# Seven half-size products in place of eight in the second MLP matmul of a fused forgetting-attention and MLP kernel

## The chip, the cores and the metric

The kernel runs on one core of one Trainium2 chip. The metric is the device time of one launch in microseconds, the median over several runs. Besides the timed runs there is one profiled execution; its rows carry the line numbers of the kernel's source (L362 is line 362), the engine (PE is TensorE's matmul, PEld its weight load, DVE is VectorE, ACT is ScalarE, POOL is GpSimd, SP is SyncE), the tile written and the tiles read.

## What is computed

```python
# attention, for each of 8 batches and 8 heads, 576 tokens, head size 64
scores = q @ k.T / sqrt(D)
decay  = cum[:, None] - cum[None, :]          # cum = cumsum(log(clip(f, 1e-4, 1)))
attn   = softmax(causal(scores + decay))
x      = (attn @ v)                           # laid out as 4608 tokens x 512
# MLP
h   = x @ w_in                                # 512 -> 2048
g   = h - tanh(h)
out = g @ w_out                               # 2048 -> 512, float32
```

## The kernel before

Matmul operands are float16 and accumulate in float32 in PSUM. The attention works on 32 pairs of heads, four pairs for each of the eight batches. The MLP works on nine units of 512 tokens (`UW`), and a unit has two stages.

- `mlp1(u, ft)`, one item for each of the 16 blocks `ft` of 128 of the 2048 hidden columns: four matmuls of 128x512 into a PSUM bank `hps` (L352), tanh by ACT into `th` (L359), and an add by DVE that leaves the float16 block `gt` of 128 hidden columns by 512 tokens (L362). `hps` comes from the pool `ps_m`, three banks in rotation, so the matmuls of a block wait until the add of the block three earlier has read its bank. `th` comes from `tmp`, two buffers.
- `mlp2(u, s)`, 16 items of four matmuls: for each of four groups of 128 tokens, 16 matmuls of 128x512 accumulate in one bank of `ps_m` over the 16 blocks (`gt` is the stationary operand, a block of `wout` the moving one, L370). After the last, ACT copies the bank to `ost` (L374), and SP's queue stores 128 rows of the output.

An item of either stage is thus four 512-column matmuls. All items stand in one list (L433), unit after unit, each unit its 16 `mlp1` and then its 16 `mlp2`:

```python
mlp = [(fn, u, s) for u in range(NU) for fn in (mlp1, mlp2) for s in range(NFT)]
take = 0 if p < NPAIR else 3 if p == NPAIR else 7 if p <= 2 * NPAIR + 1 else 8
```

The order of the work on each engine is the order in which the program writes it (`manual_schedule`), and no engine changes it. The loop goes over the pairs `p` = 0 to 32, and each pair takes `take` items of the list and spreads them evenly between its own steps. The steps of a late pair are seven score tiles (`scores`, L273 on PE, exp by ACT on L287, causal masks by POOL on L297), `values` of the pair before (30 small matmuls on L308, then three DVE operations: L318, L319, L320) and `turn` (two transposing DMAs of SP that put the result in `XR`, the input of the first MLP matmul). What is left of the list after pair 32 runs at the end by itself.

From batch 3 on, q and k are transposed by DMA and laid out by eight copies of DVE (`place`, L95), which stand in the last pair of the batch before (p = 11, 15, 19, 23, 27): two after each of the first four score tiles. For earlier batches PE transposes (L237) and DVE copies from PSUM (L248), two copies for q and two for k in each pair up to p = 10.

`XR` is a ring over tokens, 4 batches of 576 long (L67, L326). A unit whose 512 tokens cross the end of the ring does each of its `mlp1` matmuls in two parts; with this length that is unit 4 alone, in two parts of 256 columns. The blocks `gt` have 22 buffers (L57). One PSUM bank, `ps_tr`, serves the early transposes and nothing later.

The lines that the change touches are the pools (L57), the ring (L67, L326), the start-up constants (L114 to L123, L155), `mlp1` (L355), the list (L433) and `take` (L441).

## Time and profile before

| | |
|---|---|
| median of 3 runs | 362.77 us (362.58 to 364.81) |
| span of the profiled execution, first to last instruction | 359.3 us |
| the executions' time over the span, taken from these two | 3.5 us |
| PE busy | 346.5 us, 96% of the span |
| ACT busy | 221.7 us, 62% |
| DVE busy | 199.1 us, 55% |
| POOL busy | 153.6 us, 43% |

The span is the profiled execution's own time; the timed runs also hold what lies around it. A row of a timeline gives the start, the time from there to the end of the last of the merged instructions, the engine, line and shapes, the count, and in brackets how long the engine had been idle and what ended that. A row of the groups gives the count, the busy time, the mean time of one instruction in ns, and the idle time before the group's instructions. Matmuls are pipelined: one takes longer from start to end than the distance to the next, so costs of matmuls are read from the starts.

### The profile page before, as it was taken

To read this page: it belongs to the slowest core of one execution; us is meant where nothing else is said; L and a number is where in the kernel's file an instruction comes from. 1 tells how busy PE (TensorE), PEld (TensorE's weight loads), DVE (VectorE), ACT (ScalarE), POOL (GpSimd) and SP (SyncE) were. 2 spreads that over 40 slices of the span, in tenths; PEclk is the share of its full clock that TensorE was granted. 3 is DMA by queue.
4 is the path that set the end of the run, shared out by engine and by line. 5 is a ranking of instruction groups with operands and counts; after the bars stand their busy time and mean duration, and the time that the engine had idled before them with its cause. 6 is when DMAs were issued, how large, how long until landed. Compare 5 with 4: busy or idle time off the path is not lost.

```text
span 359.3 us, 7490 instructions
## 1 busy us (share of the span) xinstructions
PE 346.5 (96%) x2792; PEld 190.3 (53%) x2792; DVE 199.1 (55%) x349; ACT 221.7 (62%) x416; POOL 153.6 (43%) x316
## 2 busy tenths in 40 slices
PE   7797899999999999999999999999999999999995
PEld 3475455555555555555557865555555554444442
DVE  8666799448961577157814781378127513802710
ACT  6567676558855785578657865686568734714611
POOL 8932463766276627762776267632222210000000
PEclk9789999999999999999999999999999999999999
DMA  7999999999799999999899969991220021011011
GB/s 118 158 188 187 208 194 80 118 145 161 96 102 151 168 97 76 149 181 112 66 144 153 143 65 147 151 156 35 76 75 16 18 77 61 0 60 58 0 48 71
DMA packets 140632, 38.74 MB, mean 108 GB/s; under 512 B 128004, under 2 KB 134900, under 8 KB 140596
## 3 DMA queue, kind: packets, MB, share of 16 engines
q0 software_dynamic: 92320, 18.36, 66.7%
q1 hardware_dynamic: 48276, 19.90, 29.2%
q8 instruction: 22, 0.36, 0.4%
q14 instruction: 14, 0.11, 0.1%
HBM read 36.85 MB, written 9.44 MB: 129 GB/s over the span
## 4 chain that ended last, share of the span: by engine, by line
PE 89%; DVE 6%; ACT 2%; DMA 1%; issue 1%; ACTq 0%
PE ops L370 35%; PE hps L352 32%; PE ps L273 12%; PE av L308 8%; ACT e L287 1%; DVE gt L362 1%; DVE QT L248 1%; DMA QT<-cqs 1%; PE t L237 1%; DVE xn L320 1%; PE ps L281 1%; DVE KT L248 0%; PE spin L226 0%; DVE cum L156 0%; ACT th L359 0%
## 5 line engine op out<-in xcount | busy, mean ns | idle before, releaser
L352 PE MATMUL hps<-XR,win 128*128 128x512 f16 (+1 forms) x640 | 140.9, 357 | 0.3 <-DVE gt L362 0.2
L370 PE MATMUL ops<-wout,gt 128*128 128x512 f16 x576 | 139.2, 378 | 0.0
L287 ACT ACTIVATE e<-ps 128x512 f16<-128x512 f32 x192 | 111.0, 596 | 39.6 <-PE ps L273 26.2
L362 DVE TENSOR_TENSOR gt<-hps,th 128x512 f16<-128x512 f32 x144 | 98.5, 689 | 58.4 <-ACT th L359 57.2
L297 POOL TENSOR_SCALAR_AFFINE_SELECT e<-e 128x128 f16<-128x128 f16 x168 | 56.6, 338 | 120.8 <-ACT e L287 120.5
L359 ACT ACTIVATE th<-hps 128x512 f32<-128x512 f32 x144 | 86.3, 599 | 33.0 <-PE hps L352 31.3
L352 PEld LDWEIGHTS <-win 128*128 128x128 f16 x640 | 57.9, 97 | 48.6 <-issue 0.7
L273 PE MATMUL ps<-QT,KT 67*128 67x64 f16 (+5 forms) x384 | 77.9, 281 | 3.9 <-ACT e L287 2.1
L370 PEld LDWEIGHTS <-gt 128*128 128x128 f16 x576 | 52.0, 97 | 52.6
L273 PEld LDWEIGHTS <-KT 67*128 67x128 f16 (+1 forms) x384 | 37.7, 99 | 41.2 <-issue 2.8
L374 ACT ACTIVATE ost<-ops 128x512 f32<-128x512 f32 x36 | 21.5, 597 | 54.3 <-PE ops L370 45.3
L318 DVE TENSOR_SCALAR rs<-av 128x10 f32<-128x10 f32 (+1 forms) x33 | 5.4, 163 | 69.3 <-PE av L308 69.3
L308 PEld LDWEIGHTS <-e 128*128 128x128 f16 x896 | 32.8, 98 | 7.5 <-issue 1.7
L308 PE MATMUL av<-vn,e 128*128 128x65 f16 x896 | 34.5, 194 | 1.0 <-DVE xn L320 1.0
L106 POOL DMA_DIRECT2D vn<-in_v_dram x32 | 28.4, 898 | 1.6 <-issue 0.8
L320 DVE TENSOR_TENSOR xn<-av,rs 128x640 f16<-128x640 f32 (+1 forms) x33 | 26.5, 804 | 1.1
L248 DVE COPY KT<-t 64x576 f16<-64x576 f16 (+1 forms) x26 | 19.5, 748 | 4.5 <-PE t L237 4.3
L87 POOL DMA_DIRECT2D qn<-in_q_dram x25 | 21.5, 859 | 0.8 <-issue 0.6
L87 POOL DMA_DIRECT2D kn<-in_k_dram x25 | 21.2, 850 | 1.1 <-issue 0.9
L248 DVE COPY QT<-t 64x576 f16<-64x576 f16 x22 | 17.6, 801 | 6.5 <-PE t L237 6.3
L308 PE MATMUL av<-vn,el 128*128 128x65 f16 x64 | 12.5, 195 | 0.0
L95 DVE COPY KT<-TK 64x1152 f16<-64x1152 f16 x20 | 11.4, 607 | 0.1
(58 smaller groups left out, 127.2 us busy)
## 6 DMA issues: line engine op xcount, KB each, us to landing
out_dram<-ost SPq DMA_DIRECT2D x36, 256.0 KB
vn<-in_v_dram POOLq DMA_DIRECT2D x32, 128.0 KB, 5.9
qn<-in_q_dram POOLq DMA_DIRECT2D x20, 128.0 KB, 3.7
kn<-in_k_dram POOLq DMA_DIRECT2D x20, 128.0 KB, 4.4
win<-in_moe_w_in_dram POOLq DMA_DIRECT2D x2, 1024.0 KB, 11.8
wout<-in_moe_w_out_dram POOLq DMA_DIRECT2D x2, 1024.0 KB, 17.4
XR<-xn SPq DMA_TRANSPOSE x56
qn<-in_q_dram POOLq DMA_DIRECT2D x1, 576.0 KB, 8.9
```

Source lines behind the costliest of these rows:

```text
L87: nc.gpsimd.dma_start(out=dst[b % 2][0:pn, n, :].rearrange("p (h d) -> p h d", h=H), in_=src[b, :, n * P:n * P + pn, :].rearrange("h p d - ...
L106: nc.gpsimd.dma_start(out=vn[b % 2][:, n, h0:h1, 0:D], in_=v[b, h0:h1, n * P:(n + 1) * P, :].rearrange("h p d -> p h d"))
L248: nc.vector.tensor_copy(out=to, in_=of)
L273: nc.tensor.matmul(out=ps[:, col:col + n], lhsT=KT[b % 2][0:rows, h, j * P:(j + 1) * P], rhs=QT[b % 2][0:rows, h, i0:i0 + n], start=True, ...
L287: nc.scalar.activation(out=e[:, lo:hi], in_=ps[:, lo:hi], func=AF.Exp, scale=qscale)
L297: nc.gpsimd.affine_select(out=view, in_=view, compare_op=ALU.is_ge, fill=0.0, base=0, pattern=pat, channel_multiplier=-1)
L308: nc.tensor.matmul(out=av[:, a, ib, :], lhsT=E.pop((b, c, a, j, ib)), rhs=vn[b % 2][:, j, 2 * c + a, 0:D + 1], start=(j == 0), stop=(j == ib))
L320: nc.vector.tensor_tensor(out=xn[:, :, h0 * D:(h0 + hn) * D].rearrange("p i (a d) -> p a i d", a=hn), in0=av[:, h0:h0 + hn, :, 0:D], in1=r ...
L352: nc.tensor.matmul(out=hps[:, o:o + n], lhsT=win[:, ci, ft * P:(ft + 1) * P], rhs=XR[:, ci, t:t + n], start=(ci == 0), stop=(ci == NCH - 1))
L359: nc.scalar.activation(out=th, in_=hps, func=AF.Tanh, scale=-1.0)
L362: nc.vector.tensor_tensor(out=gt, in0=hps, in1=th, op=ALU.add)
L370: nc.tensor.matmul(out=ops, lhsT=GT[(u, ft)][:, m * P:(m + 1) * P], rhs=wout[:, ft, :], start=(ft == 0), stop=(ft == NFT - 1))
```

## The change

The second matmul of units 1 to 8 is done by the scheme of Strassen in Winograd's form, once. The hidden columns, the unit's tokens and the output columns are each cut in halves, so that `gt` gives four quarters (A11 and A21 from blocks 0 to 7, for the first and the second 256 tokens; A12 and A22 from blocks 8 to 15) and `wout` four (B11, B12, B21, B22). Seven products of quarters or of sums of quarters take the place of eight. Unit 0 keeps `mlp2`.

- Sums of `wout`: four tiles `WS`, each by two DVE operations of 128x1024 float16, one in each of tiles 1 and 4 of the pairs p = 7 to 10. The tiles serve at first as room for start-up constants (`lf`, `cum`, `minus16`, `neg16`, `tri16`, `pick_k`).
- Sums of `gt`: `mlp1` of the blocks 8 to 15 has four more DVE operations behind its add, each 128x256 float16 with both inputs in SBUF: A11-A21, A21+A22 (written over A21), S2 = (A21+A22)-A11, and A12-S2. The third reads the second's result, the fourth the third's.
- The products: `product(u, n, g)` is eight matmuls of 128x256 for one group `g` of 128 tokens. Products 1, 6, 5, 3 are accumulated one on another in one bank (`ps_tr`, `px`), which ACT copies after 1, 6 and 5 to `part` and after 3 to `ost`. Product 2 has a bank of `ps_m`; products 7 and 4 share another, one on top of the other. For 2, 7 and 4 DVE adds the bank and a `part` (128x512 float32). Each of the four results is stored as 256 rows of 256 columns.
- The list: a unit has 30 items, not 32. Block 15 of `mlp1` comes after the first half of product 1, and the others follow in the order below. Even pairs from p = 10 on take 7 items, odd ones 8. Each unit therefore takes four pairs, always with the same place: of unit u, blocks 6 to 12 lie in p = 4u+6, and blocks 13 and 14, 1a, block 15, 1b, 2a, 6a, 6b lie in p = 4u+7 (a and b are the two groups). Units 7 and 8 run at the end, after the last pair.
- The ring `XR` holds three batches, so units 3 and 6 cross its end (192+320 and 384+128 columns). `gt` has 18 buffers.

```diff
-    gtp = ctx.enter_context(tc.tile_pool(name="gtp", bufs=NFT + 6))
+    gtp = ctx.enter_context(tc.tile_pool(name="gtp", bufs=NFT + 2))
+    smp = ctx.enter_context(tc.tile_pool(name="smp", bufs=NFT // 2 + 1))
+    prt = ctx.enter_context(tc.tile_pool(name="prt", bufs=3))
...
-    RING = 4 * S
+    K2, E2, T2 = NFT // 2, DM // 2, UW // 2
+    WS = [wpl.tile([P, K2, E2], FP16, tag=f"ws{i}", name=f"ws{i}") for i in range(4)]
+    RING = 3 * S
...
-    lf = cst.tile([NH, S], FP32)
+    lf = WS[0].rearrange("p k e -> p (k e)").bitcast(FP32)[0:NH, 0:S]
+    cum = WS[1].rearrange("p k e -> p (k e)").bitcast(FP32)[0:NH, 0:S]
...
-    neg16 = cst.tile([P, P], FP16)
-    tri16 = cst.tile([P, P], FP16)
+    neg16 = WS[3].rearrange("p k e -> p (k e)")[:, 512:640]
+    tri16 = WS[3].rearrange("p k e -> p (k e)")[:, 640:768]
...
-    minus16 = cst.tile([2 * H, S], FP16)
-    pick_k = cst.tile([P, 512], FP16)
+    minus16 = WS[2].rearrange("p k e -> p (k e)")[0:2 * H, 0:S]
+    pick_k = WS[3].rearrange("p k e -> p (k e)")[:, 0:512]
...
+    for n in range(4):
+        for i in range(2):
+            LOADS.setdefault((NPAIR + 3 + n, 1 + 3 * i), []).append(lambda n=n, i=i: wsum(n, i * K2 // 2, (i + 1) * K2 // 2))
...
+    def wsum(n, k0, k1):
+        dst, a, b = ((WT1, B12, B11), (WT3, B22, B12), (WT2, B22, WT1), (WT4, B21, WT2))[n]
+        nc.vector.tensor_tensor(out=dst[:, k0:k1, :], in0=a[:, k0:k1, :], in1=b[:, k0:k1, :], op=ALU.subtract)
...
-        r0 = b % 4 * S
+        r0 = b % 3 * S
...
         nc.vector.tensor_tensor(out=gt, in0=hps, in1=th, op=ALU.add)
+        if u == 0 or ft < K2:
+            return
+        k = ft - K2
+        a1, a2 = GT[(u, k)], gt
+        sm = smp.tile([P, 3, T2], FP16, tag="sm", name="sm")
+        SUM[(u, k)] = sm
+        nc.vector.tensor_tensor(out=sm[:, 0, :], in0=a1[:, 0:T2], in1=a1[:, T2:UW], op=ALU.subtract)
+        nc.vector.tensor_tensor(out=a1[:, T2:UW], in0=a1[:, T2:UW], in1=a2[:, T2:UW], op=ALU.add)
+        nc.vector.tensor_tensor(out=sm[:, 1, :], in0=a1[:, T2:UW], in1=a1[:, 0:T2], op=ALU.subtract)
+        nc.vector.tensor_tensor(out=sm[:, 2, :], in0=a2[:, 0:T2], in1=sm[:, 1, :], op=ALU.subtract)
+
+    def product(u, n, g):
+        t0 = g * P
+        bank = {1: "X", 6: "X", 5: "X", 3: "X", 2: "W", 7: "Y", 4: "Y"}[n]
+        first = n in (1, 2, 7)
...
+        left = {1: lambda k: GT[(u, k)][:, t0:t0 + P],
+                2: lambda k: GT[(u, K2 + k)][:, t0:t0 + P],
+                3: lambda k: SUM[(u, k)][:, 2, t0:t0 + P],
+                4: lambda k: GT[(u, K2 + k)][:, T2 + t0:T2 + t0 + P],
+                5: lambda k: GT[(u, k)][:, T2 + t0:T2 + t0 + P],
+                6: lambda k: SUM[(u, k)][:, 1, t0:t0 + P],
+                7: lambda k: SUM[(u, k)][:, 0, t0:t0 + P]}[n]
+        right = {1: B11, 2: B21, 3: B22, 4: WT4, 5: WT1, 6: WT2, 7: WT3}[n]
+        for k in range(K2):
+            nc.tensor.matmul(out=ps[:, g * E2:(g + 1) * E2], lhsT=left(k), rhs=right[:, k, :],
+                             start=(first and g == 0 and k == 0), stop=(k == K2 - 1), skip_group_check=True)
+        if g == 0:
+            return
+        r0, e0 = u * UW + T2 * (n in (4, 7)), E2 * (n in (3, 7))
+        if n in (1, 6, 5):
+            part = prt.tile([P, DM], FP32, tag="part", name="part")
+            PART[(u, n)] = part
+            nc.scalar.activation(out=part, in_=ps, func=AF.Copy)
+            return
+        ost = tmp.tile([P, DM], FP32, tag="ost", name="ost")
+        if n == 3:
+            nc.scalar.activation(out=ost, in_=ps, func=AF.Copy)
+        else:
+            nc.vector.tensor_tensor(out=ost, in0=ps, in1=PART.pop((u, {2: 1, 7: 5, 4: 6}[n])), op=ALU.add)
+        nc.sync.dma_start(out=out[r0:r0 + T2, e0:e0 + E2].rearrange("(g p) e -> p g e", p=P),
+                          in_=ost.rearrange("p (g e) -> p g e", g=2))
...
-    mlp = [(fn, u, s) for u in range(NU) for fn in (mlp1, mlp2) for s in range(NFT)]
+    mlp = [(fn, 0, s) for fn in (mlp1, mlp2) for s in range(NFT)]
+    for u in range(1, NU):
+        mlp += [(mlp1, u, ft) for ft in range(NFT - 1)]
+        mlp += [(product, u, 1, 0), (mlp1, u, NFT - 1), (product, u, 1, 1), (product, u, 2, 0), (product, u, 6, 0),
+                (product, u, 6, 1), (product, u, 2, 1)]
+        mlp += [(product, u, n, g) for n in (5, 7, 3, 4) for g in range(2)]
...
-            take = 0 if p < NPAIR else 3 if p == NPAIR else 7 if p <= 2 * NPAIR + 1 else 8
+            take = 0 if p < NPAIR else 3 if p == NPAIR else 7 if p <= 2 * NPAIR + 1 or p % 2 == 0 else 8
```

More of the change, by code (lines that the diff above doesn't have):

```diff
@@ L154 @@
     nc.scalar.activation(out=first, in_=lf[0:1, 0:1], func=AF.Exp)
-    cum = cst.tile([NH, S], FP32)
     nc.vector.tensor_tensor_scan(out=cum, data0=ones16[0:NH, :], data1=lf, initial=0.0,
@@ L219 @@
                     LOADS.setdefault((p0 + 3, 2 * n + a), []).append(lambda b=b, dst=dst, src=src, a=a, c=c: place(dst, src, b, a, c))
-    E, XN, AV, HP, GT, M2 = {}, {}, {}, {}, {}, {}
+    E, XN, AV, HP, GT, M2, SUM, PART = {}, {}, {}, {}, {}, {}, {}, {}
+    B11, B12 = wout[:, 0:K2, 0:E2], wout[:, 0:K2, E2:DM]
+    B21, B22 = wout[:, K2:NFT, 0:E2], wout[:, K2:NFT, E2:DM]
+    WT1, WT2, WT3, WT4 = WS
+    def wsum(n, k0, k1):
+        dst, a, b = ((WT1, B12, B11), (WT3, B22, B12), (WT2, B22, WT1), (WT4, B21, WT2))[n]
+        nc.vector.tensor_tensor(out=dst[:, k0:k1, :], in0=a[:, k0:k1, :], in1=b[:, k0:k1, :], op=ALU.subtract)
     def spin(n):
@@ new lines, in mlp1 @@
+        nc.vector.tensor_tensor(out=sm[:, 2, :], in0=a2[:, 0:T2], in1=sm[:, 1, :], op=ALU.subtract)
[3 more added lines that the diff above has]
+        first = n in (1, 2, 7)
+        if first and g == 0:
+            if bank == "X":
+                M2[(u, bank)] = ps_tr.tile([P, DM], FP32, tag="tr", name="px")
+            else:
+                M2[(u, bank)] = ps_m.tile([P, DM], FP32, tag="m", name="pm")
+        ps = M2[(u, bank)]
+        left = {1: lambda k: GT[(u, k)][:, t0:t0 + P],
[20 more added lines that the diff above has]
+            nc.scalar.activation(out=ost, in_=ps, func=AF.Copy)
+        else:
+            nc.vector.tensor_tensor(out=ost, in0=ps, in1=PART.pop((u, {2: 1, 7: 5, 4: 6}[n])), op=ALU.add)
+        nc.sync.dma_start(out=out[r0:r0 + T2, e0:e0 + E2].rearrange("(g p) e -> p g e", p=P),
+                          in_=ost.rearrange("p (g e) -> p g e", g=2))
```

## Prediction

> **What bounds the kernel now.** I read the page first, then the chain in order of time, then the two timelines of PE and DVE that show one pair.
>
> ```profile
> span 359.3 us, 7490 instructions
> ...
> PE 346.5 (96%) x2792; PEld 190.3 (53%) x2792; DVE 199.1 (55%) x349; ACT 221.7 (62%) x416; POOL 153.6 (43%) x316
> ...
> DVE  8666799448961577157814781378127513802710
> ...
> PEclk9789999999999999999999999999999999999999
> ...
> PE 89%; DVE 6%; ACT 2%; DMA 1%; issue 1%; ACTq 0%
> ```
>
> PE carries the chain (89%), and after the start it does so at nearly full clock. But DVE's row is no flat 55%: it swings between 1 and 9 tenths within each unit, high in the first matmul's stage, low in the second's. The change gives PE less and DVE more, and most of that in the stage in which DVE is already full. So the question is not whether DVE's work fits into the span, but whether it fits where it stands.
>
> PE's prices, from the chain in order of time:
>
> ```profile
> 200.54 1.75 PE hps L352 x16
> ...
> 327.71 13.81 PE hps L352 x64
> 341.53 13.83 PE ops L370 x64
> ```
>
> 64 matmuls of 512 columns take 13.81 us, 0.216 each, so an item of four is 0.863 us. The first row is unit 4, whose blocks cross the ring's end: 16 matmuls of 256 columns, each with a weight load of its own, in 1.75 us, 0.109 each. That is the nearest row to a product's matmul. Half the columns do cost half, and that the seven products save nothing on PE is excluded.
>
> One pair on PE (the first and last row are the s0 and s1 of two pairs):
>
> ```profile
> 124.38 0.63 PE L273 MATMUL ps<-QT,KT 67*128 67x512 f16 x3
> 124.84 1.03 PE L352 MATMUL hps<-XR,win 128*128 128x512 f16 x4
> 125.71 0.58 PE L308 MATMUL av<-vn,e 128*128 128x65 f16 x14
> ...
> 126.61 1.89 PE L352 MATMUL hps<-XR,win 128*128 128x512 f16 x8
> 128.34 0.38 PE L273 MATMUL ps<-QT,KT 67*128 67x320 f16 x2
> 128.56 1.03 PE L352 MATMUL hps<-XR,win 128*128 128x512 f16 x4
> ...
> 133.60 0.63 PE L273 MATMUL ps<-QT,KT 67*128 67x512 f16 x3
> ```
>
> A pair with eight items lasts 133.60-124.38 = 9.22 us, with seven 8.36. A score tile takes 0.22 (128.34 to 128.56).
>
> **DVE's prices.**
>
> ```profile
> L362 DVE TENSOR_TENSOR gt<-hps,th 128x512 f16<-128x512 f32 x144 | 98.5, 689 | 58.4 <-ACT th L359 57.2
> L320 DVE TENSOR_TENSOR xn<-av,rs 128x640 f16<-128x640 f32 x31 | 25.6, 825 | 1.1
> L248 DVE COPY QT<-t 64x576 f16<-64x576 f16 x22 | 17.6, 801 | 6.5 <-PE t L237 6.3
> ...
> L95 DVE COPY KT<-TK 64x1152 f16<-64x1152 f16 x20 | 11.4, 607 | 0.1
> L95 DVE COPY QT<-TQ 64x1152 f16<-64x1152 f16 x20 | 10.4, 556 | 0.2
> ...
> L320 DVE TENSOR_TENSOR xn<-av,rs 128x320 f16<-128x320 f32 x2 | 1.0, 492 | 0.1
> ...
> L160 DVE SCALAR_TENSOR_TENSOR cc<-cum,cc 64x576 f16<-64x576 f32 x1 | 0.8, 753 | 0.0
> ...
> L334 DVE COPY XR<-x 128x576 f16<-128x576 f16 x1 | 0.5, 458 | 1.1 <-PE x L332 1.1
> ...
> L137 DVE MEMSET neg<- 128x64 uint32 x1 | 0.1, 112 | 0.0
> ```
>
> The two forms of L320 give a line: (825-492)/320 = 1.04 ns an element and 825-640x1.04 = 159 ns fixed. L362 lies on it (159+533 = 692). So does L160, the only other kind with both inputs in SBUF, though not all in float16: (753-159)/576 = 1.03. All-float16, dense and with one input, L334 runs at (458-159)/576 = 0.52. The trace has no float16 operation with two SBUF inputs, so a sum of 256 columns is bounded by 159+0.52x256 = 292 ns and 159+1.04x256 = 425 ns from these rows, and from below by a small fixed part: the zero fill of L137 is 112 in all, 45 beyond 64x1.04, which with 0.52 gives 180. I take 292, since the sums are dense and all float16 as L334.
>
> The Trainium skill, DVE Perf Modes ("The perf-mode tier table"), has float16-sized `tensor_tensor` at twice rate and never above, with 1224 ns for 2048 elements; an estimate from its 151 fixed cycles is 290 ns, which the sum would not notice. The same page's errata table speaks of 58 fixed cycles for SBUF operands, an estimate of 194 ns; L160's fixed part speaks against it, and what it would make of the time is the first rival below.
>
> ```profile
> 60.11 1.29 DVE L362 TENSOR_TENSOR gt<-hps,th 128x512 f16<-128x512 f32 x2
> ...
> 91.45 0.16 DVE L318 TENSOR_SCALAR rs<-av 128x10 f32<-128x10 f32 x1
> 91.64 0.22 DVE L319 RECIPROCAL rs<-rs 128x10 f32<-128x10 f32 x1
> 91.89 0.82 DVE L320 TENSOR_TENSOR xn<-av,rs 128x640 f16<-128x640 f32 x1
> 92.63 1.28 DVE L362 TENSOR_TENSOR gt<-hps,th 128x512 f16<-128x512 f32 x2
> ...
> 126.67 0.69 DVE L362 TENSOR_TENSOR gt<-hps,th 128x512 f16<-128x512 f32 x1 [0.78 <-ACT th L359]
> ...
> 176.37 2.51 DVE L95 COPY KT<-TK 64x1152 f16<-64x1152 f16 x4
> ...
> 249.90 1.75 DVE L95 COPY KT<-TK 64x1152 f16<-64x1152 f16 x4
> ...
> 327.55 13.98 PE L352 MATMUL hps<-XR,win 128*128 128x512 f16 x64
> ...
> 329.24 0.69 DVE L362 TENSOR_TENSOR gt<-hps,th 128x512 f16<-128x512 f32 x1 [13.98 <-ACT th L359]
> ```
>
> From start to start, two adds with no wait between them are 1.29-0.69 = 0.60 apart, 0.09 less than one takes; one that reads the result before it (L319, L320) starts 0.03 after its end. So a block of 8 to 15 costs DVE: add 0.60, A11-A21 0.20, A21+A22 0.32, S2 0.32, A12-S2 0.20, together 1.64 us (1.19 with 180 ns, 2.18 with 425). PE makes a block in 0.863. DVE's three operations of `values` cost 92.63-91.45 = 1.18, a `place` copy 0.44 to 0.63 (1.75 and 2.51 for four), taken at 0.55.
>
> **The change part by part.**
>
> Products: 14 items of eight 256-column matmuls, 14x0.875 = 12.25 us, for 13.82; 1.57 less a unit, **-12.6 us** for eight. All of it is on the chain.
>
> Sums of `gt`, at the end (units 7 and 8). PE takes 16 blocks in a row. The add of block 8 starts 329.24-327.55 = 1.69 after its first matmul, and that of block 15 no sooner than 7x1.64 = 11.48 later; its result is there after 0.69, at 13.86. Product 2a needs it for its last matmul. Unhindered, PE gets there after eight blocks, 1a, 1b and seven matmuls: 6.90+1.75+0.76 = 9.41. PE stands 4.4 us (partly before, where blocks 12 to 15 wait for their bank). Queued behind are 6a and all that follows. Two units: **+8.9**.
>
> In the attention (units 2 to 5, time from the start of p = 4u+6). The add of block 6 starts at 126.67-124.38 = 2.29. From there to the end of block 15's add, DVE has in its order: `values` twice 2.36, nine adds 5.40 and the last in full 0.69, seven sets of sums 7.28, and four of the eight `place` copies 2.20, together 17.9 us, with about 0.1 idle: 20.3. PE arrives at the last matmul of 2a after 8.36 and the second pair less two score tiles, two items and that matmul: 9.22-0.44-1.75-0.11 = 6.92, at 15.3. It stands 5.0 us, and so do the scores behind it, whose exps and masks were hidden until now. Four units: **+20.0**. Unit 6 has no `place`: 5.0-2.2 = **+2.8**.
>
> Unit 1 lies in p = 10 and 11, where DVE also has four copies L248 (3.2 us) and two sums of `wout` (159+0.52x1024 = 0.69 each, 1.4 us). About 1.4 of this falls into DVE's gap ahead of block 6 or beside PE's transposes: 5.0+3.2 = **+8.2**.
>
> POOL: where it is busy, DVE's copies slow down.
>
> ```profile
> 174.00:184.00 10.00, 10.00 (x80) 5.34 (x79) 6.01 (x12) 5.19 (x10) 7.00 (x13) 1.00 1.27 113
> 245.00:253.00 8.00, 8.00 (x69) 4.36 (x68) 6.41 (x14) 4.79 (x11) 2.21 (x6) 1.00 0.10 22
> ```
>
> The fifth time behind the stretch is POOL's. With POOL busy 7.0 of 10 us four copies took 2.51, with 2.2 of 8 us 1.75. The mean of the two L95 groups, 581 ns, is 10% over the 530 (0.44+0.09) of the quick four. The adds, with one SBUF input, stay at 0.69. I give the sums the same 10%: 28x0.03x6 units = **+5** (0 if they are like the adds, 28x0.19x6 = 32 if each loses all that the slow four lose). The Trainium skill, SBUF ("Who interferes with whom"), says that a DVE operation with two SBUF inputs and a GpSimd one that reads SBUF exclude each other; the rows bear out a conflict, but for copies, and no row here shows it for two inputs.
>
> Small: the second unit across the ring's end costs 16 blocks x 0.012 = **+0.2**. The order keeps the ring of three free of waits: batch b's `turn` in p = 4b+1 comes some ten items after the last block that read the same place. ACT has four copies of a bank per unit as before; each is covered by the next product in another bank. Start-up constants lie in separate columns of the shared tiles: 0 (if a tile's users waited for each other, a microsecond or two).
>
> Sum: 359.3-12.6+8.9+20.0+2.8+8.2+5+0.2 = 391.8 us of span. The median shown lies 3.5 above the span: **395**.
>
> **The rivals.**
>
> *A sum's fixed part is small* (180 ns). A block then costs 1.19, and 56 links (seven in each of eight units) give back 56x0.45 = 25, with about 3 of contention left: 368 us. For it: L137 alone. By the Trainium skill's 194 ns it would be about 371.
>
> *Full time for each element* (425 ns), as L160: 56x0.54 = 30 more, 425 us. Against it: L334.
>
> *The clock falls in the waits.* In units 1 to 5 PE waits in one piece, while DVE does two copies, `values`, an add and sums: 1.1+1.18+0.6+1.04 = 3.9 us less a few matmuls. The first slices of the page, where PE stands at times, have a clock of 7 and 8 tenths; three tenths of a 9-us slice are 2.7 us, at five places up to 13: 408 us. The Trainium skill, Matmul & The Clock Gate ("The HAM clock gate"), names an idle window of 3.4 us for it, so the wait is at the edge.
>
> *DVE keeps up* (not slower). The place is block 15's add ahead of 2a, the price the stall there; it decides by the cost of a block. All gains and losses cancel where 39.9-56x(1.64-c) = 12.4 without contention, at c = 1.15, sums of 0.14 apart. At 0.93 only unit 1 still waits (about 3), and the time is 359.3-12.4+3+3.5 = 353 us. For it: DVE's 55%. Against it: all four sums would have to follow one another faster than the zero fill's 112 ns plus the 0.03 of a dependence.
>
> **How the numbers follow.** The forecast has 0.61, the small fixed part 0.12, the clock 0.10, full time per element 0.07, DVE keeping up 0.10. The prediction is 395. The range takes in the first three, from 368 to 408, and beyond that some for dearer contention: 368 to 414; it leaves out 0.17. About 1% (3.6 us) is what a measurement can tell from no change. Faster takes most of the last case, 0.08; same its rest and the cheap end of the first rival, 0.04; slower 0.88.
>
> **What would show it.** In the profile after: idle time of PE in front of product 2a put down to DVE's `gt` or its sums, 4 to 8 us in each unit; DVE at 9 tenths through the blocks 8 to 15 with sums of 290 ns; products at 0.109 apart. Sums under 200 ns, or PE idle time elsewhere (behind `part`, `XR` or the shared bank), would make it wrong.

## The result and the profile after

| | before | after |
|---|---|---|
| median | 363.79 us (4 runs, 362.58 to 366.13) | 418.26 us (4 runs, 417.85 to 420.12) |
| span of the profiled execution | 359.3 us | 416.1 us |
| mean granted clock of PE | 0.990 | 0.932 |

The changed kernel takes 1.155 times the time, with an interval of 1.148 to 1.162. It lies 23 us over the prediction's 395 and 4 us over the top of its range. Here and below, a ratio and its interval leave out executions over 1.5% slower than the fastest of their kernel, while medians and ranges hold all of them; where the two differ, the ratio is the one to go by.

The page of the changed kernel: span, busy time, the row of DVE and of the granted clock in 40 slices, and the chain by engine.

```profile
span 416.1 us, 8663 instructions
...
PE 360.7 (87%) x3240; PEld 239.6 (58%) x3240; DVE 283.0 (68%) x637; ACT 217.9 (52%) x416; POOL 157.0 (38%) x316
...
DVE  8586896699944795369726992489437945953871
...
PEclk9599899999979996999799988999699989989998
...
PE 48%; DVE 38%; ACT 8%; issue 4%; DMA 1%; POOL 1%; ACTq 0%; DVEq 0%
```

DVE's share of the chain goes from 6% to 38%, though DVE is busy for only 68% of the span: its work falls into stretches of 9 tenths in which PE stands. And PE's busy time has risen from 346.5 to 360.7 us, although seven products take the place of eight. The row of the clock says why: it had 9 in every slice behind the start, and now drops to 6, 7 or 8 again and again.

The waits of PE, by line and by what ended them (total, times, longest):

```profile
PE pm L408 <- DVE gt L377: 33.1, 21, 3.4
PE hps L367 <- DVE gt L377: 6.2, 11, 1.1
PE ps L288 <- DVE KT L263: 3.2, 2, 1.8
```

The first is product 2a, which waits for the last `gt` blocks. One such wait, in unit 2, from the timeline of PE (start, time to the end of the last of the merged instructions, count, and in brackets the idle time before):

```profile
153.08 0.82 PE L408 MATMUL pm<-wout,gt 128*128 128x256 f16 x6 [0.48 <-DVE gt L377]
156.88 0.28 PE L408 MATMUL pm<-wout,gt 128*128 128x256 f16 x1 [2.99 <-DVE gt L377]
158.66 0.40 PE L408 MATMUL pm<-wout,gt 128*128 128x256 f16 x1 [1.50 <-DVE gt L377]
...
159.30 1.90 PE L408 MATMUL px<-ws,sm 128*128 128x256 f16 x8
```

Six of the eight matmuls run, then PE waits 2.99 us for block 14 and 1.50 us for block 15: 4.97 us with the 0.48 before, for a forecast of 5.0. But the last row was not forecast: the eight matmuls of 6a, behind the wait, take 1.90 us from first start to last end, where a product at full clock takes 1.04. The windows of the same stretch show the clock (window, its length, busy time and count of PE, PEld, DVE, ACT and POOL, granted clock, share and GB/s of the DMAs):

```profile
154.00:156.00 2.00, 0.00 (x0) 0.00 (x0) 1.92 (x6) 0.87 (x2) 1.57 (x4) 1.00 0.90 58
...
158.00:160.00 2.00, 1.34 (x7) 0.88 (x8) 1.90 (x7) 0.42 (x1) 0.00 (x0) 0.51 0.72 90
160.00:162.00 2.00, 2.00 (x11) 1.44 (x10) 1.34 (x4) 0.46 (x2) 0.42 (x1) 0.50 0.00 0
162.00:164.00 2.00, 2.00 (x11) 1.15 (x9) 0.00 (x0) 0.95 (x3) 0.41 (x1) 0.50 0.04 9
164.00:166.00 2.00, 2.00 (x34) 1.71 (x33) 0.43 (x1) 0.94 (x2) 1.01 (x2) 0.78 0.05 13
```

PE gets half its clock from 158.06 to 164.89, just when it has work again: some 6 us of work at half speed, 3 us lost. The Trainium skill, TensorE: Matmul & The Clock Gate (the section on the HAM clock gate), states that the clock halves after an idle window of about 3.4 us, that windows run free of the kernel's work, and that about as long a busy one brings the clock back. The halving agrees; the time at half clock, 6.83 us, is two such windows here, and the stretch was not wholly idle, since one matmul stands between the two waits. The last section reads the windows themselves.

The sums themselves, from the groups of DVE by form:

```profile
L387 DVE TENSOR_TENSOR sm<-gt,sm 128x256 f16<-128x256 f16 x64 | 19.4, 303 | 2.2
L384 DVE TENSOR_TENSOR sm<-gt 128x256 f16<-128x256 f16 x64 | 18.9, 296 | 0.0
L386 DVE TENSOR_TENSOR sm<-gt 128x256 f16<-128x256 f16 x64 | 18.7, 292 | 2.2
L385 DVE TENSOR_TENSOR gt<-gt 128x256 f16<-128x256 f16 x64 | 18.7, 292 | 2.2
```

A sum takes 292 to 303 ns, so the 292 of the prediction holds. How they follow one another is in DVE's timeline at the end of the kernel (unit 7), from one block's add to the next:

```profile
361.02 0.68 DVE L377 TENSOR_TENSOR gt<-hps,th 128x512 f16<-128x512 f32 x1
361.62 0.28 DVE L384 TENSOR_TENSOR sm<-gt 128x256 f16<-128x256 f16 x1
361.94 0.29 DVE L385 TENSOR_TENSOR gt<-gt 128x256 f16<-128x256 f16 x1
362.26 0.29 DVE L386 TENSOR_TENSOR sm<-gt 128x256 f16<-128x256 f16 x1
362.59 0.29 DVE L387 TENSOR_TENSOR sm<-gt,sm 128x256 f16<-128x256 f16 x1
362.80 0.68 DVE L377 TENSOR_TENSOR gt<-hps,th 128x512 f16<-128x512 f32 x1
```

A block costs 362.80-361.02 = 1.78 us, for a forecast of 1.64. The difference sits in one place: A21+A22 (L385) starts 0.32 after A11-A21 (L384), 0.04 after its end, though it reads nothing that A11-A21 writes. It was put at 0.20.

**Where the 56.8 us lie.** The first matmuls of `values` in the 10th, 12th, 28th and 32nd pair serve as marks. In the timeline of PE before:

```profile
89.46 0.58 PE L308 MATMUL av<-vn,e 128*128 128x65 f16 x14
...
107.28 0.58 PE L308 MATMUL av<-vn,e 128*128 128x65 f16 x14
...
254.83 0.58 PE L308 MATMUL av<-vn,e 128*128 128x65 f16 x14
...
290.39 0.58 PE L308 MATMUL av<-vn,e 128*128 128x65 f16 x14
```

and after:

```profile
90.12 0.58 PE L323 MATMUL av<-vn,e 128*128 128x65 f16 x14
...
120.87 0.58 PE L323 MATMUL av<-vn,e 128*128 128x65 f16 x14
...
298.41 0.58 PE L323 MATMUL av<-vn,e 128*128 128x65 f16 x14
...
337.76 0.98 PE L323 MATMUL av<-vn,e 128*128 128x65 f16 x14
```

| stretch | before | after | difference | forecast, with PE's gain of 1.57 a unit |
|---|---|---|---|---|
| up to the 10th mark | 89.46 | 90.12 | +0.7 | 0 |
| 10th to 12th (unit 1) | 17.82 | 30.75 | +12.9 | 8.2-1.6 = +6.6 |
| 12th to 28th (units 2 to 5) | 147.55 | 177.54 | +30.0 | 20.0-6.3 = +13.7 |
| 28th to 32nd (unit 6) | 35.56 | 39.35 | +3.8 | 2.8-1.6 = +1.2 |
| last mark to the end (units 7, 8) | 68.91 | 78.34 | +9.4 | 8.9-3.1 = +5.8 |

The forecast had 5 us of contention and 0.2 for the ring besides. Each unit costs more than forecast, by 1.8 us (units 7 and 8) to 6.3 (unit 1). The experiments had to find out by what.

### The profile page after: what moved, and what is told of

It is laid out like the page before. It is cut to its first block, busy times and chain, and to the rows that moved or that the text cites. A ratio compares the mean times of both kernels' runs of the same rounds, so it can differ in the third digit from the quotient of the medians.

```text
span 416.1 us, 8663 instructions
## 1 busy us (share of the span) xinstructions
PE 360.7 (87%) x3240; PEld 239.6 (58%) x3240; DVE 283.0 (68%) x637; ACT 217.9 (52%) x416; POOL 157.0 (38%) x316
## 4 chain that ended last, share of the span: by engine, by line
PE 48%; DVE 38%; ACT 8%; issue 4%; DMA 1%; POOL 1%; ACTq 0%; DVEq 0%
DVE gt L377 13%; PE px L408 13%; PE pm L408 10%; PE hps L367 8%; PE ps L288 7%; PE av L323 4%; ACT e L302 4%; DVE sm L386 4%; DVE gt L385 4%; DVE sm L387 4%; ACT th L374 3%; PE ops L432 3%; DVE sm L384 3%; DVE xn L335 3%; DVE QT L99 2%
## 5 line engine op out<-in xcount | busy, mean ns | idle before, releaser
L367 PE MATMUL hps<-XR,win 128*128 128x512 f16 (+4 forms) x704 | 144.0, 342 | 6.6 <-DVE gt L377 6.2
L312 POOL TENSOR_SCALAR_AFFINE_SELECT e<-e 128x128 f16<-128x128 f16 x168 | 59.9, 359 | 159.1 <-ACT e L302 159.0
L367 PEld LDWEIGHTS <-win 128*128 128x128 f16 x704 | 62.4, 97 | 55.9 <-issue 10.8
L288 PE MATMUL ps<-QT,KT 67*128 67x64 f16 (+5 forms) x384 | 81.7, 298 | 6.3 <-DVE KT L263 3.2
L408 PEld LDWEIGHTS <-gt 128*128 128x128 f16 x512 | 49.8, 101 | 48.2 <-DVE gt L377 34.7
L422 DVE TENSOR_TENSOR ost<-pm,part 128x512 f32<-128x512 f32 x24 | 16.5, 689 | 57.5 <-PE pm L408 50.7
L408 PE MATMUL pm<-wout,gt 128*128 128x256 f16 x128 | 22.7, 308 | 33.1 <-DVE gt L377 33.1
L408 PEld LDWEIGHTS <-sm 128*128 128x128 f16 x384 | 41.1, 110 | 11.8 <-issue 2.1
L416 ACT ACTIVATE part<-px 128x512 f32<-128x512 f32 x24 | 14.4, 598 | 40.4 <-PE px L408 40.4
L408 PE MATMUL px<-ws,sm 128*128 128x256 f16 x128 | 26.9, 385 | 0.0
L263 DVE COPY KT<-t 64x576 f16<-64x576 f16 (+1 forms) x26 | 19.4, 747 | 3.9 <-PE t L252 3.7
## 6 DMA issues: line engine op xcount, KB each, us to landing
wout<-in_moe_w_out_dram POOLq DMA_DIRECT2D x2, 1024.0 KB, 17.2
```

Of the source, the lines that this page charges most:

```text
L263: nc.vector.tensor_copy(out=to, in_=of)
L288: nc.tensor.matmul(out=ps[:, col:col + n], lhsT=KT[b % 2][0:rows, h, j * P:(j + 1) * P], rhs=QT[b % 2][0:rows, h, i0:i0 + n], start=True, ...
L312: nc.gpsimd.affine_select(out=view, in_=view, compare_op=ALU.is_ge, fill=0.0, base=0, pattern=pat, channel_multiplier=-1)
L367: nc.tensor.matmul(out=hps[:, o:o + n], lhsT=win[:, ci, ft * P:(ft + 1) * P], rhs=XR[:, ci, t:t + n], start=(ci == 0), stop=(ci == NCH - 1))
L408: nc.tensor.matmul(out=ps[:, g * E2:(g + 1) * E2], lhsT=left(k), rhs=right[:, k, :], start=(first and g == 0 and k == 0), stop=(k == K2 - ...
```

## The experiments

The theory: two things are missing in the sum, 0.14 us in each of 56 blocks (7.8 us), because A21+A22 waits for A11-A21 to have read A21 before it writes over it, and the halved clock behind the long waits (about 3 us in each of units 1 to 5, less in unit 6). The rivals: the sums are slowed in some other way (by POOL, by their number), the 0.14 is a wait for the add of the block and not for A11-A21, or part of the loss comes from elsewhere (products, bank, ring, shared tiles).

### The sums left out

```diff
-        sm = smp.tile([P, 3, T2], FP16, tag="sm", name="sm")
...
-        nc.vector.tensor_tensor(out=sm[:, 2, :], in0=a2[:, 0:T2], in1=sm[:, 1, :], op=ALU.subtract)
...
-                3: lambda k: SUM[(u, k)][:, 2, t0:t0 + P],
+                3: lambda k: GT[(u, K2 + k)][:, t0:t0 + P],
...
-                6: lambda k: SUM[(u, k)][:, 1, t0:t0 + P],
-                7: lambda k: SUM[(u, k)][:, 0, t0:t0 + P]}[n]
+                6: lambda k: GT[(u, k)][:, T2 + t0:T2 + t0 + P],
+                7: lambda k: GT[(u, k)][:, t0:t0 + P]}[n]
```

The four sums of `gt` are not computed; products 3, 6 and 7 read quarters of `gt` instead.

> Left out: the four sums of each block 8 to 15, 64 sets in all; products 6, 7 and 3 read blocks of gt in their place, so PE's, ACT's and the DMA's work is that of the changed kernel. If DVE's queue is what costs (the forecast's mechanism), PE keeps its 12.6 us and little is lost: a span of about 348 (359.3-12.6+0.2 and about 1 at the start), 351 to 352 us, PE without waits at product 2. If the products themselves are dear (weight loads, the waits of the chained bank for its copies, the output in 1 KB rows), it stays well above 360.

353.69 us, beside 363.16 of the kernel before: 0.974 (0.967 to 0.981). No wait for `gt` in product 2a is left among PE's longest. The sums' price is thus 418.3-353.7 = 64.6 us, where the prediction had 8.9+20.0+2.8+8.2+5 = 44.9 (unit 1's sums of `wout` among it, which this kernel still does). All that is wrong by more than a few us lies in the sums and in what they cause; the products, the chained bank and the ring of three cost nothing of that size. The gain of PE was put at 12.6; this shows 9.5.

### The clock held up

```diff
+        fill = {6: 12, 7: 5} if u <= 5 else {6: 6, 7: 5} if u == 6 else {6: 3, 7: 5}
...
+            if (n, g) == (2, 0) and k in fill:
+                t32 = ps_sc.tile([P, 512], FP32, tag="sc", name="fill")
+                for _ in range(fill[k]):
+                    nc.tensor.matmul(out=t32, lhsT=ones16[:, 0:P], rhs=ones16[:, 0:UW])
```

PE does matmuls that nobody reads in the waits ahead of the last two matmuls of product 2a. The waits stay as long as DVE makes them.

> Dummy matmuls (512 columns, into a score bank that nobody reads) stand in the two waits of product 2a, ahead of its last two matmuls: 12 and 5 in units 1 to 5, 6 and 5 in unit 6, 3 and 5 in units 7 and 8; nothing else is changed. They fit into time in which PE stands. If the halved clock behind the wait is a cost of its own, the granted clock stays at 1.00 and about 3 us come back in each of units 1 to 5 and 1.5 to 2 in units 6 and 7: 18 us, about 400 us. If the lower clock falls into time that is lost to DVE anyway, the time stays at 418.

401.05 us: 1.103 (1.097 to 1.109), and 17.2 us less than the changed kernel, at a mean clock of 0.982 for 0.932. The windows of the same stretch in this kernel:

```profile
156.00:158.00 2.00, 1.58 (x14) 1.19 (x14) 1.90 (x7) 0.60 (x1) 0.17 (x1) 1.00 0.78 94
158.00:160.00 2.00, 2.00 (x20) 1.62 (x19) 1.35 (x4) 1.52 (x3) 0.91 (x2) 1.00 0.02 5
```

The clock stays at 1.00 through the place where it was 0.51 and 0.50, and PE does 20 matmuls between 158 and 160, not 7. More matmuls make the kernel faster: of the 23 us that the prediction lacked, 17 are the clock. By the marks, the pair with product 2a is 2.9 to 3.1 us shorter in each of units 1 to 5, 1.1 in unit 6, and the end 2.1.

### A11-A21 one block earlier

```diff
-        if u == 0 or ft < K2:
+        if u == 0 or ft < K2 - 1:
...
+        if ft < NFT - 1:
+            nx = smp.tile([P, 3, T2], FP16, tag="sm", name="sm")
+            SUM[(u, k + 1)] = nx
+            b1 = GT[(u, k + 1)]
+            nc.vector.tensor_tensor(out=nx[:, 0, :], in0=b1[:, 0:T2], in1=b1[:, T2:UW], op=ALU.subtract)
+        if k < 0:
+            return
+        a1, a2, sm = GT[(u, k)], gt, SUM[(u, k)]
```

The same four sums in the same place, but the A11-A21 behind a block's add belongs to the next block. A21+A22 still follows an add and another operation; it no longer follows the one that reads what it overwrites.

> A11-A21 of a block is done one block earlier, so that A21+A22, which writes over A21, no longer stands right behind the operation that reads A21. If that write is what makes it wait (A21+A22 starts 0.03 after the end of A11-A21 in the changed kernel, not 0.09 before), a block falls from 1.78 to 1.64 us and 56 links give 7.8 us: about 410, less if a wait gets short enough for the clock to hold. If it waits for gt's add instead, it starts where it does now and the time stays at 418.

407.90 us (403.76 to 409.66): 1.120 (1.112 to 1.128), 10.4 less than the changed kernel. DVE's timeline at the end:

```profile
350.14 0.68 DVE L377 TENSOR_TENSOR gt<-hps,th 128x512 f16<-128x512 f32 x1
350.74 0.28 DVE L385 TENSOR_TENSOR sm<-gt 128x256 f16<-128x256 f16 x1
350.94 0.28 DVE L389 TENSOR_TENSOR gt<-gt 128x256 f16<-128x256 f16 x1
...
351.80 0.68 DVE L377 TENSOR_TENSOR gt<-hps,th 128x512 f16<-128x512 f32 x1
```

A21+A22 (now L389) starts 0.20 after the operation before it, and the block costs 351.80-350.14 = 1.66: the 1.64 of the prediction to within rounding. It reads the same fresh `gt` as ever, so a wait for the add is excluded; what cost 0.12 was that an operation writes where the one directly before it reads. 56x0.12 = 6.7 of the 10.4 us are that wait. The rest goes with the clock: the changed kernel's profile lacks 28.3 us of full clock (6.8% of 416.1), this one's 24.3 (6.0% of 405.5). About half of this difference lies in the attention, behind shorter waits, the other half in the first 50 us, where executions of one kernel differ too.

### Sums spread over all blocks

```diff
-        mlp += [(mlp1, u, ft) for ft in range(NFT - 1)]
+        mlp += [(mlp1, u, ft) for ft in (0, 1, 2, 8, 3, 9, 4, 10, 5, 11, 6, 12, 7, 13, 14)]
```

Blocks 8 to 12 are made early, so that blocks with sums alternate with blocks without. The number of operations is the same.

> Order of the blocks in the first matmul: 0, 1, 2, 8, 3, 9, 4, 10, 5, 11, 6, 12, 7, 13, 14, then 1a and 15 as before. The work is the same, but the sums are spread over 13 blocks, not 8. If the queue on DVE sets the wait, two sets of sums fewer lie in the last two pairs: the wait of units 1 to 6 falls from about 6.0 to 3.5 us, at the end (units 7 and 8) from 5.4 to 4.1. That is 18 us: 400 us if the clock still falls, about 385 if the shorter wait lets it hold. If the order does not matter (DVE's total does), it stays near 418.

399.88 us: 1.098 (1.091 to 1.105). PE's waits in product 2a fall from 33.1 to 19.1 us, and those of `hps` rise from 6.2 to 10.0. The rest of the 18.4 us gained is clock (0.946) and the tail. Position alone, with the clock that hangs on it, is thus worth 18 us, and DVE's total work is not what bounds the kernel; but two waits of 1.67 and 1.49 us in unit 2 are enough for the clock to fall again.

### Both of the prediction's conditions restored

The edits of the second and the third experiment together, with fewer matmuls in the shorter waits:

```diff
+        fill = {6: 9, 7: 5} if u <= 5 else {6: 4, 7: 5} if u == 6 else {6: 2, 7: 5}
```

> Both edits together: dummy matmuls in the waits of product 2a (9 and 5, 4 and 5, 2 and 5, since the waits are shorter here) and A11-A21 one block ahead. This gives the forecast its two conditions back, a clock that holds and a block at 1.64 us. If these two were all that it had wrong, the time is that of e2_fill less 56x0.14 = 7.8 us, 393 us, beside the forecast of 395. If a third cost of several us is at work in the waits, it stays at 398 or above.

395.70 us (392.54 to 396.25): 1.087 (1.082 to 1.092). With the pitch of a block as the prediction had it and PE at full clock, the time comes out at the 395 of the prediction. That it does so to within 1 us is partly luck: the 5 us of contention are not there, and unit 1 and a smaller gain of PE take their place (below).

### Sums late, apart and wide

```diff
-        gt = gtp.tile([P, UW], FP16, tag="gt", name="gt")
+        if ft % 4 == 0:
+            G4[(u, ft // 4)] = gtp.tile([P, 4, UW], FP16, tag="gt", name="gt")
+        gt = G4[(u, ft // 4)][:, ft % 4, :]
...
+        if u > 0 and ft == NFT - 1:
+            sums12(u, 1)
...
+        nc.vector.tensor_tensor(out=s1, in0=quarter(u, "21", j), in1=quarter(u, "22", j), op=ALU.add)
+        nc.vector.tensor_tensor(out=s2, in0=s1, in1=quarter(u, "11", j), op=ALU.subtract)
...
+        if (n, g) == (1, 0):
+            sums12(u, 0)
+        elif (n, g) == (6, 0):
+            sum3(u, 0)
+            sum3(u, 1)
+        elif (n, g) == (6, 1):
+            sum4(u, 0)
+            sum4(u, 1)
...
-        mlp += [(product, u, 1, 0), (mlp1, u, NFT - 1), (product, u, 1, 1), (product, u, 2, 0), (product, u, 6, 0),
-                (product, u, 6, 1), (product, u, 2, 1)]
+        mlp += [(product, u, 1, 0), (mlp1, u, NFT - 1), (product, u, 1, 1), (product, u, 2, 0), (product, u, 2, 1),
+                (product, u, 6, 0), (product, u, 6, 1)]
```

Four blocks of `gt` share a tile, and a sum is one operation of 128x1024 over four blocks, 8 a unit in place of 32. S1 = A21+A22 and S2 stand behind 1a and behind block 15's add, A11-A21 (`sum3`) at 6a, A12-S2 (`sum4`, written over A12) at 6b. S1 has a tile of its own, and 2b comes ahead of 6a and 6b, because A12-S2 is written over A12, which product 2 reads.

> The same sums and products, but the sums are taken out of the stretch in which PE waits for gt: eight DVE operations of 128x1024 for a unit (four blocks at a time) in place of 32 of 128x256, the first two behind block 14, two behind block 15, four beside products 6a and 6b; products in the order 1, 2, 6, 5, 7, 3, 4, so that four halves of products that need no sum stand ahead of the first that does. Nothing on DVE then stands between gt's adds. If the order on DVE is the cause, PE hardly waits and the time is near that of e1_no_sums (353.7): 354 to 358, faster than before. If DVE's added time in total is what costs, or the long waits only move to product 6a, it stays above 363.

362.71 us (12 runs, 361.51 to 364.92): 1.000 (0.997 to 1.003). The loss of 55 us is gone, but of the gain of PE nothing is left either: the expectation of 354 to 358 was missed. Where the rest goes is in PE's timeline (here `gt` is written in L379, and products are L427):

```profile
143.90 0.28 PE L427 MATMUL pm<-wout,gt 128*128 128x256 f16 x1 [0.87 <-DVE gt L379]
...
294.75 1.91 PE L427 MATMUL px<-ws,sm 128*128 128x256 f16 x16 [0.68 <-ACT part L435]
```

Product 2a still waits, for block 15's add, which now stands behind S1 and S2 of the first half. And in the units at the end product 5 waits 0.68 for ACT to copy the bank that 6 and 5 share.

### The start-up alone

```diff
-    RING = 4 * S
+    RING = 3 * S
...
-    lf = cst.tile([NH, S], FP32)
+    lf = WS[0].rearrange("p k e -> p (k e)").bitcast(FP32)[0:NH, 0:S]
...
-        r0 = b % 4 * S
+        r0 = b % 3 * S
```

The kernel before, with the ring of three and the start-up constants in the shared tiles, nothing else. The start of the kernels differs by some us between executions (the fifth pair's `values` at 43.7 us before, 45.7 after, up to 49.2 in other kernels), which could be a cost of the shared tiles.

> The kernel before, with the change's shared tiles for the start-up constants and its ring of three batches, and nothing else. In the profiles of the changed kernels the fifth pair's values come 1 to 3 us later than in the one before. If the shared tiles (or the ring) cause that, this kernel takes 364.5 to 366 us; if it is the transfers at the start, which differ from one execution to the next, it stays within 1 us of 363.

364.64 us (12 runs, 360.88 to 366.25): 1.002 (0.999 to 1.005). A cost of 1 us is neither shown nor excluded, one of 2 us is excluded. The scatter, in which single executions of one kernel differ by up to 5 us, isn't explained by these edits. It goes with the clock: in the first 50 us of the profiled execution PE has half its clock for 6.8 us in the kernel before and for 20.5 in this one, and of the 23 executions of the kernel before, the three with a mean clock of 0.990 took 360.71 to 362.49 us, the four with 0.974 took 363.06 to 365.43.

### Four small operations for a wide one

```diff
-        nc.vector.tensor_tensor(out=s1, in0=quarter(u, "21", j), in1=quarter(u, "22", j), op=ALU.add)
-        nc.vector.tensor_tensor(out=s2, in0=s1, in1=quarter(u, "11", j), op=ALU.subtract)
+        for i in range(4):
+            nc.vector.tensor_tensor(out=SUM[u][:, 0, 4 * j + i, :], in0=quarter(u, "21", j)[:, i, :], in1=quarter(u, "22", j)[:, i, :], op=ALU.add)
+        for i in range(4):
+            nc.vector.tensor_tensor(out=SUM[u][:, 1, 4 * j + i, :], in0=SUM[u][:, 0, 4 * j + i, :], in1=quarter(u, "11", j)[:, i, :], op=ALU.subtract)
```

The kernel with late sums, but each sum in four operations of 128x256 (the same for `sum3` and `sum4`), four of a kind in a row, so that none waits for the one before it.

> As e6_late_wide, but with the 32 operations of 128x256 for a unit that the change has, four of a kind one behind the other, so that each reads what lies four operations back. If only the order counts, a sum costs DVE 0.20 us from start to start (no wait for the one before) and eight take 1.6 us, four wide ones 2.8 for the same blocks: block 15's add comes no later than in e6_late_wide by more than 0.3 us, and the time is within 2 us of its 362.7. If the many small operations are what was dear in the change, each unit loses about 1 us more: 370.

369.01 us (365.24 to 373.03): 1.009 (1.005 to 1.014), where the wide sums had 1.000 (0.997 to 1.003). So the number of operations counts by itself, some 3.5 us by the ratios, and place and order are the other 52 us of the 55.5 between the kernel with late wide sums and the changed one. PE's waits in product 2a are 7.6 us, 4.6 with wide sums.

### Sums spread between the early blocks

```diff
+        if 1 < u < 7 and ft in (9, 11, 12):
+            (lambda: sum3(u, 0), lambda: sum3(u, 1), lambda: sums12(u, 0))[(9, 11, 12).index(ft)]()
...
-        if (n, g) == (1, 0):
+        apart = 1 < u < 7
+        if (n, g) == (1, 0) and not apart:
...
-        mlp += [(product, u, n, g) for n in (5, 7, 3, 4) for g in range(2)]
+        mlp += [(product, u, n, g) for n, g in ((7, 0), (5, 0), (5, 1), (7, 1), (3, 0), (3, 1), (4, 0), (4, 1))]
...
+                    if (whole, len(mine)) == (9, 7) and n == 4:
+                        break
```

The kernel with late wide sums, and in units 2 to 6 three groups of sums moved up between the blocks, as soon as their quarters are there; 7a comes ahead of 5a, so that ACT's copy of the shared bank lies beside a product; and pairs of seven items put no two score tiles side by side.

> As e6_late_wide, with what is still late there moved: in units 2 to 6 three of the wide sums' pairs behind blocks 9, 11 and 12 (nothing of the sums ahead of block 15's add), 7a between 6b and 5a and 7b behind 5b (a product in another bank while ACT copies the chained one, 0.68 us of waiting a unit), and in pairs with seven items one item behind the third score tile instead of two behind the values (0.2 us in two pairs of four). A unit then loses about 0.1 us, not 1.0 in the attention and 0.8 at the end: 352 to 356 us, 2 to 3% faster than before. If DVE's total work in these pairs binds, it stays within 1% of 363.

361.51 us (356.53 to 362.94): 0.990 (0.983 to 0.996), not the 352 to 356 expected. The bank and the score tiles came out as meant (a pair of seven items lasts 8.4 us for 8.6), but the pair with product 2a still takes 10.8, worse than the 10.3 with late wide sums. Sums, `place` copies and `values` now follow one another on DVE ahead of the last adds, and PE waits 0.86 us for block 14 and 0.31 for block 15 (unit 2), where it waited 0.87 for block 15 alone.

### The same, three blocks earlier

```diff
-        if 1 < u < 7 and ft in (9, 11, 12):
-            (lambda: sum3(u, 0), lambda: sum3(u, 1), lambda: sums12(u, 0))[(9, 11, 12).index(ft)]()
+        if 1 < u < 7 and ft in (5, 8, 11):
+            (lambda: sum3(u, 0), lambda: sum3(u, 1), lambda: sums12(u, 0))[(5, 8, 11).index(ft)]()
```

> As e8_spread, with the three early pieces of the sums of units 2 to 6 behind blocks 5, 8 and 11, not 9, 11 and 12, so that DVE enters the pair with the q and k copies without a backlog. In e8_spread's trace that pair still lasts 10.8 us in units 2 to 5 (9.25 in e1_no_sums), since block 13's add starts 1.1 us late behind the sums and the copies. If that backlog is what is left, the pair falls to 9.3 to 9.8 and the time by 4 to 6 us: 355 to 358. If the copies alone fill DVE there, it stays at 361.

356.58 us (355.71 to 358.68), beside 363.23: 0.983 (0.978 to 0.988), 1.2 to 2.2% faster than the kernel before the change. The page, and the wait of product 2a in PE's timeline:

```profile
span 354.0 us, 8474 instructions
...
PE 336.6 (95%) x3240; PEld 229.6 (65%) x3240; DVE 258.6 (73%) x445; ACT 220.1 (62%) x416; POOL 164.1 (46%) x316
...
DVE  8757799668999379937892799379937863883781
...
PEclk9679999999999999999999999999999999999999
...
PE 74%; DVE 18%; ACT 3%; issue 2%; DMA 1%; POOL 0%; DVEq 0%; POOLq 0%; ACTq 0%
```

```profile
143.38 0.28 PE L432 MATMUL pm<-wout,gt 128*128 128x256 f16 x1 [0.31 <-DVE gt L379]
```

The 4.97 us that PE stood ahead of product 2a in this unit are 0.31 (the pair still lasts 9.84 us, 9.26 without sums), the clock has no hole left behind the start, and PE is busy for 336.6 us, 9.9 less than before. DVE still has 258.6 us of work for the changed kernel's 283.0, and a higher share of the span (73% for 68%). So its total never bound the kernel; what stood ahead of block 15 did.

## Why the prediction was wrong, point by point

**What held.** The mechanism and the place: PE stands ahead of the last matmuls of product 2a, for DVE's `gt`, with DVE at 9 tenths, and the rival that DVE keeps up is out. The price of a sum: 292 to 303 ns for a forecast of 292, so the rivals "a sum's fixed part is small" (180) and "full time for each element" (425) fall. The Trainium skill, VectorE: DVE Perf Modes (the perf-mode tier table), has twice the rate for such an operation, and its estimate of 290 ns agrees. The products: 16 of them follow in 1.75 us in the tail (376.78 to 378.53 in PE's timeline), 0.109 each. The wait in unit 2: 4.97 us for 5.0, though this is partly luck. With the block at 1.78 the same reckoning gives 5.0+7x0.14 = 6.0, and the sums' whole price in units 2 to 5, with the clock held up, is 5.8 us each (165.6 us between the 12th and the 28th mark, 142.6 without sums).

**The clock was a rival and not a term; this is the step that failed.** The prediction named the fall of the clock, found a wait of "3.9 us less a few matmuls" for units 1 to 5, called it "at the edge" and gave it 0.10. Holding the clock up gave 17.2 us back (prediction: up to 13). The size at one place was nearly right (2.7 us for 3). The judgement whether it happens was not: the step weighed the longest wait by itself, where two waits with one matmul of 0.1 us between them acted together (2.99 and 1.50 us in unit 2), and it stopped at unit 5, though waits of 1.71 and 1.49 us in unit 6 and of 0.97 and 1.50 us in unit 7 were enough (why, the last section shows). So 17.2 us that the runs show stand in the sum as nothing.

**The block was put at 1.64, and took 1.78.** The prediction had "A21+A22 0.20", the distance of two operations that don't wait for one another, because it looked for what A21+A22 reads. It is written over A21, which the operation before it reads, and so it waits as for a result. With 56 links that is 7.8 us. The experiment with A11-A21 a block earlier restored 1.66.

**Unit 1: +12.9 for a forecast of +6.6.** Some 3.1 of the difference are the clock and 7x0.14 = 1.0 the block. In the place of the other 2.2, PE's timeline has waits that the prediction did not look for:

```profile
95.42 1.02 PE L367 MATMUL hps<-XR,win 128*128 128x512 f16 x4 [1.10 <-DVE gt L377]
...
100.61 0.61 PE L288 MATMUL ps<-QT,KT 67*128 67x512 f16 x3 [1.75 <-DVE KT L263]
```

The copies of the transposed keys (L263) stand behind the sums on DVE, so the first score tile of the next pair waits 1.75 us for them, long before product 2a. The prediction had added up these copies only as work ahead of block 15. The first wait, 1.10 us, is no matter of the sums of `gt`: it stands in the kernel without them too, where unit 1 takes 19.47 us, 1.7 more than before the change and not some 1.6 less. How much of the 2.2 us each of the two waits makes isn't shown.

**Units 2 to 5: +30.0 for +13.7.** The clock gives 11.9 of the 16.3 that lack, the block 4x0.98 = 3.9; what is left is within what these marks can tell. **Unit 6:** 1.1 for the clock and 1.0 for the block, of 2.6. **The end:** 2.1 and 2.0, for 3.6.

**Contention was put at +5 and is about 1.** The four sums' means add up to 1183 ns, 15 more than 4x292, in 64 blocks: 1.0 us. With POOL idle, in units 7 and 8, the four have medians of 282 to 293 ns, and in the attention 280 to 293. `place`'s copies are even quicker than before (449 and 522 ns for 607 and 556). The Trainium skill, SBUF — State Buffer ("Who interferes with whom"), says that a DVE operation with two SBUF inputs contends with a GpSimd operation that reads SBUF; with POOL busy for 38% of the span, the sums' 292 to 303 ns leave room for little of it.

**The gain of PE: 12.6 forecast, 9.5 shown** by the kernel without sums. Four pairs of it last 35.65 us on average in units 2 to 5, 1.24 less than the 36.89 before and not 1.57. In a pair of seven items two score tiles came to stand side by side, and the next waits for its exp: the pair lasts 8.57 us, not the 8.36 of the prediction, and with the tiles apart 8.4.

The differences of the stretches add up: 0.7+6.3+16.3+2.6+3.6 is 29.5 over the forecast, less the 5.2 of contention and ring that it had besides, 24.3 us: from a span of 391.8 to the 416.1 measured. That the time misses by 23 and not by 24 comes from the 3.5 us put on top of the span, which mixed two executions: an execution here takes 1.7 us longer than its own span (417.85 us for 416.1).

## What to carry to other kernels

Before adding work to an engine with idle time, list what stands behind each added instruction in its queue, and when the bounding engine needs that: over the kernel without them, the sums cost 64.6 us behind the adds that are waited for, and some 3 us (356.6-353.7) some blocks earlier in wider operations, or a little more, since that kernel also has the gain from moving a product and a score tile. Where a forecast has PE stand for some us in each round, the clock behind the wait belongs in the sum as a term of its own, and two waits with hardly any work between them can count as one. Of two operations in a row ask also what the second writes, since overwriting what the first reads costs as much as reading its result.

## What the runs showed of the hardware

Whether the clock falls isn't set by the length of the wait alone. Units 7 and 8 have the same waits in PE's timeline, to the hundredth:

```profile
367.10 0.28 PE L408 MATMUL pm<-wout,gt 128*128 128x256 f16 x1 [0.97 <-DVE gt L377]
368.88 0.28 PE L408 MATMUL pm<-wout,gt 128*128 128x256 f16 x1 [1.50 <-DVE gt L377]
...
400.30 0.28 PE L408 MATMUL pm<-wout,gt 128*128 128x256 f16 x1 [0.97 <-DVE gt L377]
402.08 0.28 PE L408 MATMUL pm<-wout,gt 128*128 128x256 f16 x1 [1.50 <-DVE gt L377]
```

Behind them, in the same timeline, the 16 matmuls of product 6 take 2.95 us in unit 7, and in unit 8 1.91, at full clock. What differs is where the waits lie on a grid of time. By the trace's record of the clock, it falls from the 10th mark on at 113.69, 158.06, 202.43, 246.81, 291.18, 335.55 and 369.69 us, each a multiple of 3.413 us from the others, and returns one or two such steps later. The windows between the points of this grid, for PE alone (window, its length, busy time and count of PE, granted clock, share and GB/s of the DMAs):

```profile
366.27:369.69 3.42, 1.09 (x9) 1.00 0.00 0
369.69:373.10 3.41, 3.41 (x19) 0.50 0.00 0
...
396.99:400.41 3.42, 2.45 (x19) 1.00 0.00 0
400.41:403.82 3.41, 1.91 (x17) 1.00 0.02 5
403.82:407.23 3.41, 3.41 (x34) 1.00 0.16 58
```

Both waits of unit 7 lie in one window, those of unit 8 in two. From the 10th mark on, a window at full clock with PE busy for 0.28 to 1.45 us is each time followed by half clock, and one with 1.80 or more never. Full clock comes back only behind a window in which PE was busy throughout: those with 2.67 to 2.91 us, right behind the waits of units 1 to 5, did not bring it back. The edge isn't sharp (with A11-A21 one block earlier, a window with 1.82 us was followed by half clock), and the ends of matmuls are modelled. The free-running window of the Trainium skill, TensorE: Matmul & The Clock Gate (the section on the HAM clock gate), would give this, with the phase of the window deciding, and the trace agrees. So the same two waits, 2.5 us in all, cost the clock in unit 7 and not in unit 8, and for such waits a forecast that doesn't know the phase can only give a chance. In units 1 to 5 the phase makes no difference: however the 4.5 us of the last two waits lie on the grid, one window holds at least half of them, and PE is busy in it for less than 1.45 us (an estimate from these rows).

On DVE, an operation that overwrites what the one directly before it reads starts 0.03 to 0.04 us after that one's end, as one that reads its result does; without such a tie it starts about 0.08 before that end (0.20 behind one of 0.28).
